# One stretch of hand order around the first expert, and later transposes for the next slot, in a fused attention and two-layer mixture kernel

## The chip, the cores and the metric

One Trainium2 chip, one of its cores. The metric is device time in microseconds (us) of one execution; lower is better.

## The reference, cut to what matters

```python
scores = cap * tanh(q @ k.T / sqrt(D) / cap)         # 4 batches, 12 heads, 448 tokens, D = 64
x = softmax(scores) @ v                              # 1792 tokens x 768
h = x @ w_in                                         # 768 -> 1024
x = layernorm(h * softmax(h)) * g_ln @ w_out         # 1024 -> 768
logits = x @ w_gate + modality_bias[modality_id]     # 8 experts
e_idx, gate = argmax(logits), its softmax weight
for e in range(8):                                   # only the chosen expert of each token
    out[e_idx == e] = gate * (relu(x @ w1[e]) @ w2[e])
```

## The kernel before, in words

Three parts follow one another on TensorE (PE): attention, the dense layer, and the routed experts. Products in full precision are made as three products of rounded halves (a high part `..h` and a low part `..l`), so each weight block needs two operations after its load: a cast on ScalarE (ACT) gives the high part, a subtraction on VectorE (DVE) the low part.

The experts run in slots. The first slot, **E**, takes 256 tokens of the expert that was most frequent in the early tokens, and it starts while the routing of the last tokens is being finished. Its first product is `e_h` (L1037): 6 blocks of the contraction times 8 column groups f times 3 matmuls, 144 in all. The sums lie in two tiles of PSUM, `e_ph0` (f 0 to 3) and `e_ph1` (f 4 to 7). In the last block, after each pair of column groups, ACT takes `e_hh = relu(e_ph)` (L1055) and DVE `e_hl` (L1056). Its second product is `e_o` (L1058): 8 steps f of 12 matmuls each, into the two tiles `e_po`. The weights of E come through `e_weights` (L1026): SyncE (SP) loads a block into `e_raw` (three buffers), ACT casts it (L1033), DVE subtracts (L1034). The second product has eight such blocks, k 0 to 7; block k 7 loads into the buffer that block k 4 leaves.

The next slot, **D**, takes 512 tokens of one expert. Four gathers on GpSimd (POOL) fetch its tokens (`ygD`, L1197). `s_tr` (L1203) transposes one of the four tiles with six PE transposes into two PSUM tiles `xtD` (L1219); ACT copies each to `xh_D` (L1220) and DVE makes `xl_D` (L1221). The pool `psT` for `xtD` has two buffers, so the next tile's transposes need the `xl_D` of the tile before. D's weight blocks are loaded by SP into `raw_D` (four buffers), and `c_split` (L1178) makes `wh_D` (ACT, L1188) and `wl_D` (DVE, L1189). A small slot **T** of 32 tokens runs inside D; its tokens are scaled on DVE (`t_sc`, L1338 to L1340) and then transposed on PE (`t_tr`, L1347).

All this is interleaved with `e_o` by `lead` (L1530): `e_o` calls `step(f)` ahead of the twelve matmuls of f. There `advance()` issues the next loads of D's weights and splits one block, and `tr(i)` makes the transposes of D's tile i (i = 4: `t_sc`, `t_tr` and one gather of T). `LTR` says at which f which `tr` is made.

The order of an engine's instructions comes from one of two sources. Inside `tc.manual_schedule(...)` the engines that are named (all, if none is named) keep the order in which the code is written. Outside, and on engines that are not named, a planner orders them by costs of its own. Each `manual_schedule` block is a stretch of its own, and the planner may interleave two neighbouring stretches. Before the change, the tail of the routing, all of `e_h` and E's weights form a stretch with hand order for PE and DVE alone, so ACT and SP are planned there. From `e_o` on, a second stretch has hand order on all engines:

```python
    with tc.manual_schedule(engines={ET.PE, ET.DVE}):
        ...
        for _ in eh:          # 102 matmuls of e_h that are left, with e_hh and e_hl
            pass
        for _ in ew:          # blocks k 4 to 7 of E's second product
            pass
    ...
    with tc.manual_schedule():
        next(slots)           # gathers and first loads of D, then lead
```

Of the kernel before, what the change touches and what calls it, by code (L numbers as in the profile page):

```python
# [25 lines left out]
ND = DM // P  # L26
# [12 lines left out]
COL0 = {"D": 0, "F": 16, "H": 32, "T": 40}  # L39
TT = 32  # L40
EARLY = 10
LTR = (2, 3, 4, 5, 7)
ENDS = (3, 4)
TAIL = (12, 12, 10)
NS = NK * len(KINDS)
# [41 lines left out]
def attn_moe_kernel(ctx, tc, qt, kt, vv, cap, w_in, w_out, g_ln, ids, w_gate, mbias, w1, w2, out):  # L87
# [949 lines left out]
    def e_h():  # L1037
        xh, xl = ee["xh"], ee["xl"]
        ph = []
        hh, hl = ([mp.tile([P, 4, SLOT], F32R, tag="m4", name=f"e_{x}{q}", bufs=4) for q in range(2)] for x in ("hh", "hl"))  # L1040
        ee["hh"], ee["hl"] = hh, hl
        for d in range(ND):
            for f in range(NF):
                if d == 0 and f % 4 == 0:
                    ph.append(atile(f"e_ph{f // 4}").rearrange("p a (b c) -> p (a b) c", c=SLOT))
                o = ph[f // 4][:, f % 4, :]
                c = slice(f * P, (f + 1) * P)
                pe.matmul(o, winh[d][:, c], xh[:, d, :], start=(d == 0 and f % 2 == 0), stop=False, skip_group_check=True)
                yield
                pe.matmul(o, winh[d][:, c], xl[:, d, :], start=False, stop=False, skip_group_check=True)  # L1050
                yield
                pe.matmul(o, winl[d][:, c], xh[:, d, :], start=False, stop=(d == ND - 1), skip_group_check=True)
                if d == ND - 1 and f % 2:
                    q, r = f // 4, slice(f % 4 - 1, f % 4 + 1)
                    act.activation(hh[q][:, r, :], ph[q][:, r, :], AF.Relu)  # L1055
                    dve.scalar_tensor_tensor(hl[q][:, r, :], ph[q][:, r, :], 0.0, hh[q][:, r, :], op0=ALU.max, op1=ALU.subtract)  # L1056
                yield
    def e_o(step):  # L1058
        po = [atile(f"e_po{i}") for i in range(2)]
        for f in range(NF):  # L1060
            step(f)
            for i in range(2):
                o = slice(i * P, (i + 1) * P)
                hh, hl = ee["hh"][f // 4][:, f % 4, o], ee["hl"][f // 4][:, f % 4, o]
                for hf in range(2):
                    c = slice(hf * HD, (hf + 1) * HD)
                    p = po[i][:, hf, :HD]
                    pe.matmul(p, hh, wouh[f][:, c], start=(f == 0), stop=False)
                    pe.matmul(p, hh, woul[f][:, c], start=False, stop=False)
                    pe.matmul(p, hl, wouh[f][:, c], start=False, stop=(f == NF - 1))  # L1070
        for i in range(2):
            ob = g2.tile([P, DM], F32, tag="tm", name=f"e_ob{i}", bufs=NTM)
            act.activation(ob[:, :HD], po[i][:, 0, :HD], AF.Copy, scale=ga0[:, i:i + 1])
            dve.tensor_scalar(ob[:, HD:], po[i][:, 1, :HD], ga0[:, i:i + 1], None, op0=ALU.mult)
            pool.indirect_dma_start(out=oview("E", i), out_offset=IndirectOffsetOnAxis(ap=sidx0[:, i:i + 1], axis=0),
                                    in_=ob, in_offset=None, bounds_check=NT, oob_is_err=False)
# [18 lines left out]
    def run(k):  # L1095
        for _ in range(k):
            msteps.pop(0)[1]()

    def run_h(k):
        for _ in range(k):  # L1100
            next(eh)

    def weights():
        yield from ee["w0"]
        yield from e_weights(1)

    with tc.manual_schedule(engines={ET.PE, ET.DVE}):
        run(4)
        ra, rb = (route_group(K, rt, psR, atile, *x) for x in groups)
        ew = weights()  # L1110
        next(ra)
        next(ew)
        run(5)
        next(ra)
        run(3)
        next(rb)
        next(ew)
        run(3)
        next(ra, None)
        run(3)  # L1120
        next(rb)
        next(rb)
        next(ew)
        run(4)
        eh = e_h()
        for steps, subs in EHS:
            run_h(steps)
            next(rb, None)
            for _ in range(subs):
                next(ew)  # L1130
        for _ in eh:
            pass
        for _ in ew:
            pass
    for pl_ in (rt, xp, wi, psR):
        pl_.release()

# [251 lines left out]
    def run_slots(seq, small, lead=None):  # L1389
# [63 lines left out]
        if lead:  # L1453
            lead(advance, first)
        else:
            s_tr(seq[0])
# [73 lines left out]
    def lead(advance, tr):  # L1530

        def step(f):
            if f < ND:
                advance()
            if f in LTR:
                tr(LTR.index(f))

        late["ps"] = psT
        e_o(step)
        for pl_ in (psT, psA, mp, wo):  # L1540
            pl_.release()
        late["g1"] = tc.alloc_tile_pool(name="g1", bufs=1, reuse_waits="tile")
        late["ps"] = tc.alloc_tile_pool(name="psC", bufs=8, space=PSUM, reuse_waits="tile")

    slots = run_slots(STATIC, SMALL, lead)
    with tc.manual_schedule():
        next(slots)
        more = nc.values_load(nsl[0:1, 4:5], min_val=0, max_val=4 * NK * len(KINDS))
        next(slots)
# [56 lines left out]
```

## Time and profile before

| | |
|---|---|
| median of 3 runs | 763.64 us |
| lowest run | 762.24 us |
| profiled execution | 764.74 us |
| span of the profile | 763.0 us |
| PE busy | 728.3 us (95% of the span) |
| DVE, ACT, POOL busy | 438.5, 387.2, 117.1 us |
| mean granted clock of PE | 0.982 |

The span goes from the first to the last instruction; the profiled execution's own time has 1.74 us around it. The granted clock is a share of 2.4 GHz: 1.00 is that level, 0.50 is 1.2 GHz. All times below count from the start of the span.

### The profile page before, as it was taken

How to read it: one execution, taken by the hardware profiler on the slowest of the kernel's cores; microseconds unless marked ns; L12 is line 12 of the kernel's file. 1: busy time of each engine (PE TensorE's matmuls, PEld its weight loads, DVE VectorE, ACT ScalarE, POOL GpSimd, SP SyncE). 2: the span in 40 equal slices, each digit the busy share in tenths (PEclk: the TensorE clock that was granted, in tenths of full speed). 3: DMA queues.
4: the chain of work that ended last, by engine and by line, in shares of the span. 5: the costliest groups of instructions: out<-in, count | busy, mean ns of one | idle time of the engine just before them, and what ended most of it. 6: DMA issues, size and time to landing. Idle time of an engine off the chain costs nothing. (4 is left out here: it accounts for less than half of the span.)

```text
span 763.0 us, 11321 instructions
## 1 busy us (share of the span) xinstructions
PE 728.3 (95%) x4302; PEld 560.6 (73%) x4302; DVE 438.5 (57%) x782; ACT 387.2 (51%) x535; POOL 117.1 (15%) x214
## 2 busy tenths in 40 slices
PE   6999999999999999999999999759999999999994
PEld 2434556666777777777698998759879998799983
DVE  7999556756655657554557458456147163563621
ACT  5899756775565555556522234234145162553530
POOL 4121101112021012111032111301200220002010
PEclk9999999999999999999999999978999999999998
DMA  9675211120121110100004022747927459584530
GB/s 303 233 248 184 61 57 47 56 80 36 37 82 37 58 57 28 44 34 13 22 21 146 22 77 70 234 160 252 383 85 247 154 158 395 221 259 163 204 107 22
DMA packets 33425, 97.13 MB, mean 127 GB/s; under 512 B 4903, under 2 KB 11057, under 8 KB 33362
## 3 DMA queue, kind: packets, MB, share of 16 engines
q1 hardware_dynamic: 26546, 66.88, 25.9%
q0 software_dynamic: 6528, 29.42, 10.9%
q8 instruction: 35, 0.57, 0.3%
q14 instruction: 28, 0.23, 0.1%
q10 hardware_dynamic: 288, 0.03, 0.0%
HBM read 85.24 MB, written 11.27 MB: 126 GB/s over the span
## 5 line engine op out<-in xcount | busy, mean ns | idle before, releaser
L735 ACT ACTIVATE e<-sc,sc 112x896 f32<-112x896 f32 x96 | 94.5, 1004 | 68.6 <-PE sc L728 68.6
L740 ACT ACTIVATE e<-e,cap_t 112x896 f32<-112x896 f32 x96 | 98.2, 1046 | 1.7
L770 PE MATMUL av<-e,v 112*64 112x448 f32 x384 | 83.3, 555 | 0.0
L650 PE MATMUL y<-wouh,lh 128*128 128x392 f32 (+1 forms) x224 | 77.9, 348 | 0.5 <-DVE lg L654 0.5
L652 PE MATMUL y<-wouh,ll 128*128 128x392 f32 (+1 forms) x224 | 75.8, 338 | 0.1
L651 PE MATMUL y<-woul,lh 128*128 128x392 f32 (+1 forms) x224 | 75.9, 339 | 0.0
L595 PE MATMUL h<-winh,xh 128*128 128x512 f32 x168 | 69.0, 410 | 0.0
L597 PE MATMUL h<-winh,xl 128*128 128x512 f32 x168 | 66.0, 393 | 1.1 <-DVE xl L583 1.1
L596 PE MATMUL h<-winl,xh 128*128 128x512 f32 x168 | 65.7, 391 | 0.0
L770 PEld LDWEIGHTS av<-e,v 112*64 112x64 f32 x384 | 23.3, 136 | 35.4 <-issue 33.1
L650 PEld LDWEIGHTS y<-wouh,lh 128*128 128x128 f32 x224 | 42.0, 188 | 9.1 <-issue 7.1
L1189 DVE TENSOR_TENSOR wl_H<-raw_H,wh_H 128x768 fp32r<-128x768 f32 (+1 forms) x28 | 29.2, 1069 | 32.9 <-ACT wh_H L1188 32.8
L595 PEld LDWEIGHTS h<-winh,xh 128*128 128x128 f32 x168 | 31.6, 188 | 16.5 <-issue 9.3
L1318 PE MATMUL poD<-wh_D,hhD 128*128 128x384 f32 x128 | 43.0, 336 | 0.0
L1319 PE MATMUL poD<-wl_D,hhD 128*128 128x384 f32 x128 | 42.8, 334 | 0.0
L1320 PE MATMUL poD<-wh_D,hlD 128*128 128x384 f32 x128 | 42.8, 334 | 0.0
L652 PEld LDWEIGHTS y<-wouh,ll 128*128 128x128 f32 x224 | 42.1, 188 | 0.8 <-DVE ll L640 0.8
L651 PEld LDWEIGHTS y<-woul,lh 128*128 128x128 f32 x224 | 42.1, 188 | 0.6
L1188 ACT CAST wh_H<-raw_H 128x768 fp32r<-128x768 f32 (+1 forms) x28 | 25.3, 943 | 33.1 <-PE phD L1246 15.2
L1189 DVE TENSOR_TENSOR wl_D<-raw_D,wh_D 128x768 fp32r<-128x768 f32 (+1 forms) x28 | 29.8, 1071 | 21.3 <-ACT wh_D L1188 21.1
L597 PEld LDWEIGHTS h<-winh,xl 128*128 128x128 f32 x168 | 31.5, 188 | 8.8 <-DVE xl L583 2.0
L1188 ACT CAST wh_D<-raw_D 128x768 fp32r<-128x768 f32 (+1 forms) x28 | 26.0, 931 | 23.6 <-DMA raw_D<-in_w_dram 23.4
(373 smaller groups left out, 1613.9 us busy)
## 6 DMA issues: line engine op xcount, KB each, us to landing
rawc<-in_w_out_dram POOLq DMA_DIRECT2D x16, 384.0 KB, 4.5
rawc<-in_w_in_dram POOLq DMA_DIRECT2D x12, 512.0 KB, 4.8
raw_D<-in_w_dram SPq DMA_DIRECT2D x12, 512.0 KB, 5.5
wr_T<-in_w_dram SPq DMA_DIRECT2D x16, 384.0 KB, 6.4
raw_D<-in_w_dram SPq DMA_DIRECT2D x16, 384.0 KB, 5.1
wr_T<-in_w_dram SPq DMA_DIRECT2D x12, 512.0 KB, 7.6
raw_H<-in_w_dram SPq DMA_DIRECT2D x12, 512.0 KB, 6.1
raw_H<-in_w_dram SPq DMA_DIRECT2D x16, 384.0 KB, 3.8
```

Source lines behind the costliest of these rows:

```text
L595: pe.matmul(o, s["xh"][d], winh[d][:, c], start=(d == 0), stop=False)
L596: pe.matmul(o, s["xh"][d], winl[d][:, c], start=False, stop=False)
L597: pe.matmul(o, s["xl"][d], winh[d][:, c], start=False, stop=(d == ND - 1))
L650: pe.matmul(o, s["lh"][f], wouh[f][:, c], start=(f == 0), stop=False)
L651: pe.matmul(o, s["lh"][f], woul[f][:, c], start=False, stop=False)
L652: pe.matmul(o, s["ll"][f], wouh[f][:, c], start=False, stop=(f == NF - 1))
L735: act.activation(e, t[:CK, :, :S], AF.Tanh, scale=sc8[:CK])
L740: act.activation(e, e, AF.Exp, scale=cap_t[:CK])
L770: pe.matmul(o[64 * j:64 * j + 64, :S], v[:, c, 64 * j:64 * j + 64], et[b, p, c][:, j, :], start=(c == 0), stop=(c == 3))
L1188: act.copy(h_, raw)
L1189: dve.tensor_sub(l_, raw, h_)
L1318: pe.matmul(p, hh[:, f, o], wh[:, c], start=(f == 0), stop=False)
```

## The change

The rest of `e_h` and of E's weights leaves the stretch with hand order on PE and DVE and opens the stretch with hand order on all engines, which then runs on without a break through `e_o` and the slots. In `lead`, D's four tiles are transposed at f = 3, 4, 5, 6 (before: 2, 3, 4, 5), T at 7 as before. `advance()` now stands behind `tr` and not ahead of it, and is called at f = 3 to 7 (five blocks) and not at f = 0 to 5 (six blocks).

```diff
-LTR = (2, 3, 4, 5, 7)
+LTR = (3, 4, 5, 6, 7)
...
-        for _ in eh:
-            pass
-        for _ in ew:
-            pass
+    hand = ExitStack()
+    hand.enter_context(tc.manual_schedule())
+    for _ in eh:
+        pass
+    for _ in ew:
+        pass
     for pl_ in (rt, xp, wi, psR):
         pl_.release()
...
         def step(f):
-            if f < ND:
-                advance()
             if f in LTR:
                 tr(LTR.index(f))
+            if f >= LTR[0]:
+                advance()
...
     slots = run_slots(STATIC, SMALL, lead)
-    with tc.manual_schedule():
+    with hand:
         next(slots)
```

## Rows read from the trace of the kernel before

**Rows 1.** Waits of PE, whole span: us in total, times, longest.

```profile
PE xtD L1219 <- DVE xl_D L1221: 8.5, 1, 8.5
...
PE e_po L1068 <- ACT e_hh L1055: 4.8, 1, 4.8
PE poH L1320 <- PEq L1558: 1.1, 1, 1.1
```

**Rows 2.** Timeline of PE, 490 to 496: start, us, operation, [idle before <-releaser].

```profile
490.53 0.28 PE L1050 MATMUL e_ph<-e_xl,winh 128*128 128x256 f32 x1
490.65 0.28 PE L1052 MATMUL e_ph<-e_xh,winl 128*128 128x256 f32 x1
495.74 0.69 PE L1068 MATMUL e_po<-wouh,e_hh 128*128 128x384 f32 x1 [4.82 <-ACT e_hh L1055]
```

**Rows 3.** Timeline of PE, 515 to 532.

```profile
515.52 1.54 PE L1219 MATMUL xtD<-ident,ygD 128*128 128x128 f32 x6 [8.45 <-DVE xl_D L1221]
...
520.64 0.82 PE L1219 MATMUL xtD<-ident,ygD 128*128 128x128 f32 x6
...
523.42 0.82 PE L1219 MATMUL xtD<-ident,ygD 128*128 128x128 f32 x6
...
530.71 0.34 PE L1069 MATMUL e_po<-woul,e_hh 128*128 128x384 f32 x1
...
531.06 0.39 PE L1245 MATMUL phD<-xh_D,wh_D 128*128 128x512 f32 x1
```

**Rows 4.** Timeline of PE's weight loads, around 496.

```profile
496.47 0.29 PEld L1048 LDWEIGHTS e_ph<-e_xh,winh 128*128 128x128 f32 x1 [0.23 <-DVE e_hl L1056]
```

**Rows 5.** Timeline of ACT, 494 to 522.

```profile
494.36 0.83 ACT L1033 CAST wouh<-e_raw 128x768 fp32r<-128x768 f32 x1 [1.68 <-DMA e_raw<-in_w_dram]
495.10 0.59 ACT L1055 ACTIVATE e_hh<-e_ph 128x512 fp32r<-128x512 f32 x1
...
507.43 0.83 ACT L1033 CAST wouh<-e_raw 128x768 fp32r<-128x768 f32 x1 [4.74 <-DMA e_raw<-in_w_dram]
508.78 1.05 ACT L1188 CAST wh_D<-raw_D 128x1024 fp32r<-128x1024 f32 x1 [0.52 <-DMA raw_D<-in_w_dram]
...
513.65 0.85 ACT L1220 CAST xh_D<-xtD 128x384 fp32r<-128x384 f32 x2
...
521.91 1.07 ACT L1188 CAST wh_D<-raw_D 128x1024 fp32r<-128x1024 f32 x1
```

**Rows 6.** Timeline of DVE, 495 to 527.

```profile
495.72 0.69 DVE L1056 SCALAR_TENSOR_TENSOR e_hl<-e_ph,e_hh 128x512 fp32r<-128x512 f32 x1 [10.10 <-ACT e_hh L1055]
...
503.33 2.68 DVE L1034 TENSOR_TENSOR woul<-e_raw,wouh 128x768 fp32r<-128x768 f32 x3
...
521.68 1.02 DVE L1221 TENSOR_TENSOR xl_D<-xtD,xh_D 128x384 fp32r<-128x384 f32 x2 [1.89 <-ACT xh_D L1220]
...
523.01 1.23 DVE L1189 TENSOR_TENSOR wl_D<-raw_D,wh_D 128x1024 fp32r<-128x1024 f32 x1 [0.25 <-ACT wh_D L1188]
...
525.67 0.11 DVE L1338 TENSOR_SCALAR gtT<-ygT 32x1 f32<-32x1 f32 x1
...
526.00 0.61 DVE L1340 TENSOR_SCALAR ygT<-ygT,gtT 32x768 f32<-32x768 f32 x1
```

**Rows 7.** Loads of E's weights: ns min/median/max, first and last issue.

```profile
L1031 SPq DMA_DIRECT2D e_raw<-in_w_dram x14: 332/333/374, 405.5 to 504.4; - x14
```

**Rows 8.** Loads of D's weights, all slots D: time to landing.

```profile
DMA to landing us min/median/max: 3.4/5.3/8.7
```

**Rows 9.** Windows: length, busy and count of PE, PEld, DVE, ACT, POOL; granted clock, DMA share, GB/s.

```profile
26.00:27.00 1.00, 1.00 (x8) 0.20 (x8) 1.00 (x4) 1.00 (x2) 0.38 (x1) 0.50 1.09 432
...
747.00:748.00 1.00, 0.48 (x3) 0.51 (x4) 0.00 (x0) 0.00 (x0) 0.00 (x0) 1.00 0.07 16
```

**Rows 10.** Windows of the D slot, columns as in rows 9.

```profile
552.00:554.00 2.00, 2.00 (x11) 1.65 (x10) 0.10 (x1) 1.05 (x1) 0.00 (x0) 1.00 1.02 412
...
558.00:560.00 2.00, 2.00 (x10) 1.65 (x10) 0.21 (x1) 0.76 (x2) 0.00 (x0) 1.00 0.01 4
```

## The prediction

> **What bounds the kernel now.** PE is busy for nearly the whole span, so only time that PE loses can be won. I read the list of PE's waits first: apart from the first load of the kernel, two entries matter, one of 8.5 us and one of 4.8 us, and both lie where the change works [rows 1]. Then the timeline of PE around them, for what stood in front and how fast PE ran behind, and last the timelines of the engines named as releasers.
>
> The first loss: after the 126th of `e_h`'s 144 matmuls (start 490.65) the next thing PE does is a matmul of `e_o` at 495.74, which waited 4.82 us for `e_hh` [rows 2]. `e_hh` could have run at 491, but on ACT it stands behind three casts of E's weights, the last of which itself waited for its load and started at 494.36; `e_hh` follows at 495.10 [rows 5]. The planner had put the casts first, since ACT is free of hand order there.
>
> The second: at f = 3 PE stands 8.45 us before D's second transposes, until `xl_D` of the first tile has freed the PSUM tiles; PE goes on at 515.52 [rows 3]. That `xl_D` waits for `xh_D` at 513.65, which on ACT is behind the casts of D's blocks 0 to 2 [rows 5], because `advance()` was called at f = 0, 1, 2 ahead of `tr(0)`. Those casts waited for loads: SP could issue them only behind E's last block (504.4) [rows 7], and that one only when DVE's subtraction of block k 4 (first of the three at 503.33 [rows 6]) had freed its buffer. So the late `e_hh` delays D's loads too.
>
> After either wait PE runs at the lower clock for a while: from 515.52 to 520.64 for six transposes and twelve matmuls that take 2.78 from 520.64 to 523.42 [rows 3], a loss of 2.34.
>
> **What can be won at most.** From 490.77 (where matmul 127 would have started: spacing 0.12, rows 2) to D's first product at 531.06 [rows 3] are 40.3 us. The work in it at full rate: 18 matmuls of `e_h` x 0.118 = 2.1; three steps f of `e_o` without transposes, 12 x 0.175 (two matmuls from 530.71 to 531.06, rows 3) = 2.1 each, 6.3; five steps with transposes, 2.78 each, 13.9. Sum 22.3, so 18.0 us are lost: 4.8 + 8.45 + 2.3 and, by difference, 2.4 behind the first wait.
>
> **What the change makes of it, part by part.**
>
> *One stretch on all engines.* ACT now takes the four `e_hh` ahead of the casts k 4 to 7. The 4.8 us go. But the planner could interleave two stretches, and within one it can't. Rows 4 show why it had moved two `e_o` matmuls into `e_h`: the next `e_h` matmul (f = 2, other bank of the same tile `e_ph0`) has a wait on `e_hl` of f = 0, 1; its weight load started 0.06 us after that `e_hl` ended (495.72 + 0.69 [rows 6]; 496.47 [rows 4]). In hand order nothing stands between. So PE stops at f = 2 of the last block and, in the other tile, at f = 6. Price of one: last matmul ends 490.93, `e_hh` 0.05 later, from its start to the weight load 1.37 (495.10 to 496.47), matmul 0.1 later, about 492.45 against 490.77: 1.65 us. Two: **3.3 us**. Bounds: 0, if the second is hidden by DVE and ACT order, to 3.6.
>
> Then `e_h` ends and `e_o` starts at 490.77 + 2.1 + 3.3, about 496.3. Its f = 0 needs the first `e_hh`, `e_hl`, long done. E's blocks: casts k 4 to 6 have their loads (the last cast began at 494.36 in the trace); they start behind the last `e_hh` at about 497.1. The subtraction of k 4 ends at 498.8 (2.68 for three, rows 6), SP issues k 7 at 498.9 and it lands 3.0 later (504.4 to 507.43, rows 5 and 7), at 501.9; its subtraction ends near 503.7, while `e_o` needs it at f = 7. No wait there, with some ten us of cover.
>
> *D's loads and transposes.* SP's first loads of D follow k 7; the first landed 4.4 after k 7's issue (508.78 [rows 5]), so now at 503.3 instead of 508.8. `tr(0)` comes at f = 3: 496.3 + 6.3 = 502.5. Per step f I take offsets from T, the start of its transposes (520.64 in the trace): `xl_D` at 1.04 to 2.06, cast of D's block from 1.27, subtraction 2.37 to 3.60 [rows 5, 6]. `xl_D` of tile 0 waits for k 7's subtraction and ends near 504.7; `tr(1)` is due at 505.3. Later steps come every 2.78 and each `xl_D` is done by T + 2.06: no PE wait as long as the subtraction (T + 3.60) leaves DVE before the next `xl_D` is due (T + 3.82). It does, by 0.2 us.
>
> *The move of `advance()` behind `tr`.* This has a price at f = 7, where `tr(4)` scales T's tokens on DVE before PE can transpose them. In the trace DVE was free for that at 525.67, long before. Now the subtraction of D's block 3, issued at f = 6, stands ahead: it ends at T6 + 3.60, the three T operations take 0.94 (525.67 to 526.61, rows 6), so T's transposes can start at T6 + 4.55 against T7 = T6 + 2.78: **1.8 us**, with the rest of `e_o` queued behind. Bounds 0 and 3 (a late block 3). The sixth block moves into D's first product, where it is needed five blocks later; nothing waits.
>
> *Behind `e_o`.* D starts at 496.3 + 6.3 + 13.9 + 1.8 = 518.3. T's blocks (SP) are released by `e_o`'s steps and so come earlier with them; D's blocks 4 and 5 fall 1 to 3 us later against `e_o`'s end. DMA is full there (share 1.02 at 552) but idle again at 558 [rows 10], and PE waited for no load in that slot [rows 1]. The two blocks are 1 MB, 2.5 us at the 412 GB/s of rows 10; I take 0, and 2.5 as the bound if the cover were gone.
>
> **Sum.** 18.0 - 3.3 - 1.8 = 12.9, rounded by the walk to 531.06 - 518.3 = 12.8. Profiled execution 764.74 - 12.8 = 751.9; it lay 1.1 above the median of 763.64, so on that scale **750.8 us**, 1.7% less. About 2% (15.3 us) is what a measurement of this kernel can tell from no change; the forecast is within it.
>
> **Rivals.** *The short stops cost the clock.* After the long waits PE came back at half rate and lost 2.3 to 2.4 each time. Against: a stop of 1.1 us near the end [rows 1] left the clock at 1.00 [rows 9]. For: at 26 the clock stood at 0.50 though PE shows no long gap [rows 9], and here two stops of 1.65 lie 1.4 us apart. One fall gives 753.1, a second, at f = 7, 755.5.
> The Trainium skill (TensorE: Matmul & The Clock Gate, "A second HAM failure mode: psum-queue depth-cycling") says that short idles of PE between groups of matmuls, from waiting for PSUM, can keep the clock going up and down; by that rule this rival is the likely one, and the trace has no such pair of stops to test it.
>
> *The stops are smaller.* If the waits at `e_ph` are not there, 747.5; if only T's is not, 749.0; neither, 745.7. For: the wait at f = 6 was already over when PE came to it in the trace. Against: rows 4.
>
> *D's loads come late and hold the transposes (the other side).* Place: ACT's cast of D's block 0 ahead of `xh_D` of tile 1. It must land by 504.7, 1.4 after my estimate; from there each us is a us of PE at `tr(2)`. With the longest landing of the trace, 8.7 [rows 8], it lands near 508.1: 754.2. Slower than before it gets from 12.8 us late on, at 517.5, twice the longest landing: possible only if the order on SP is otherwise than I read.
>
> *Nothing moves.* The planner keeps the casts ahead of `e_hh`, and the wait stays: 763.6.
>
> **How the numbers follow.** Forecast (749.5 to 752.5) 0.52; smaller stops 0.18; clock 0.18; late loads 0.08, of it 0.02 above 763.6; nothing moves 0.04. The range 747.5 to 755.5 takes in both stops' bounds and two falls of the clock. Faster by over 2% means below 748.4: most of the smaller stops, 0.15. Slower by over 2%: 0.02. Within: 0.83.
>
> **What would show it.** `e_hh` on ACT at 491, ahead of the three casts; two PE waits of about 1.5 for `e_hl`; D's loads from 499; no PE wait for `xl_D`; one of 1.8 at T's transposes; granted clock 1.00 through; D's product at 518. I am wrong if the `e_ph` waits are missing, if the clock falls, or if `xl_D` appears in the waits again.

## The result and the profile after

The changed kernel takes 752.36 us (median of 4 runs, 751.36 to 753.62) against 763.64 for the kernel before (median of 3 runs, 762.24 to 763.99), 11.3 less: ratio 0.9858, 95% interval 0.9834 to 0.9882. That is a gain of 1.2 to 1.7%, less than 2%. The forecast was 750.8, in a range of 747.5 to 755.5. The profiled execution took 751.36, its span 749.6 (before: 763.0). A fourth run of the kernel before, at 1039 us, is far off the others and is in no comparison.

The list of PE's waits in the changed kernel behind the kernel's first load, as in [rows 1] (us in total, times, longest):

```profile
PE e_ph L1048 <- DVE e_hl L1056: 2.8, 2, 1.4
PE tpT L1349 <- issue: 1.6, 1, 1.6
```

The two large waits of [rows 1] are gone, for `e_hh` (4.8) and for `xl_D` (8.5). In their place stand two stops for `e_hl` and one at T's transposes. PE's timeline, which answers to [rows 2 and 3]:

```profile
472.44 0.29 PE L1048 MATMUL e_ph<-e_xh,winh 128*128 128x256 f32 x1
...
488.84 0.28 PE L1052 MATMUL e_ph<-e_xh,winl 128*128 128x256 f32 x1
490.53 0.39 PE L1048 MATMUL e_ph<-e_xh,winh 128*128 128x256 f32 x1 [1.41 <-DVE e_hl L1056]
...
493.63 0.39 PE L1048 MATMUL e_ph<-e_xh,winh 128*128 128x256 f32 x1 [1.41 <-DVE e_hl L1056]
...
503.45 0.82 PE L1221 MATMUL xtD<-ident,ygD 128*128 128x128 f32 x6
504.03 0.42 PE L1068 MATMUL e_po<-wouh,e_hh 128*128 128x384 f32 x1
...
506.22 0.90 PE L1221 MATMUL xtD<-ident,ygD 128*128 128x128 f32 x6
...
511.64 0.34 PE L1070 MATMUL e_po<-wouh,e_hl 128*128 128x384 f32 x1
513.62 0.53 PE L1349 MATMUL tpT<-ident,ygT 32*128 32x32 f32 x6 [1.65 <-issue]
514.08 0.44 PE L1068 MATMUL e_po<-wouh,e_hh 128*128 128x384 f32 x1
...
517.63 0.60 PE L1247 MATMUL phD<-xh_D,wh_D 128*128 128x512 f32 x1
```

The steps with D's transposes follow one another without a stop (503.45, 506.22: 2.77). T's transposes stop PE, and the last twelve matmuls behind them are slow: 514.08 to 517.63 is 3.55, against 2.2 for the twelve from 504.03 to 506.22. The granted clock in windows shows why (columns as in [rows 9]):

```profile
26.00:27.00 1.00, 1.00 (x10) 0.16 (x8) 1.00 (x4) 1.00 (x2) 0.45 (x1) 1.00 1.05 414
512.00:514.00 2.00, 0.38 (x6) 0.41 (x6) 1.45 (x4) 0.00 (x0) 0.00 (x0) 1.00 0.87 238
514.00:516.00 2.00, 2.00 (x10) 1.96 (x9) 0.52 (x1) 1.31 (x3) 0.92 (x1) 0.66 0.97 389
516.00:518.00 2.00, 2.00 (x7) 1.96 (x7) 1.24 (x2) 0.66 (x2) 0.48 (x1) 0.50 1.03 413
546.00:548.00 2.00, 2.00 (x11) 1.65 (x10) 1.44 (x3) 1.75 (x4) 0.00 (x0) 1.00 0.01 2
```

The first row answers to the 0.50 at 26 in [rows 9]: here the clock stood at 1.00, and `e_h` begins 1.8 us earlier. Most of that is there long before the code that was changed: the dense layer's first matmul starts at 96.9, before at 98.6. It is why these two spans differ by 13.4 and the medians only by 11.3. The first matmul of `e_h` in the kernel before:

```profile
474.22 0.28 PE L1048 MATMUL e_ph<-e_xh,winh 128*128 128x256 f32 x1
```

For comparisons between profiles I therefore use the length from the first matmul of `e_h` to D's first product, called the **E-to-D length** below: before 474.22 to 531.06, 56.8; after 472.44 to 517.63, 45.2; **11.65 less**, close to the 11.3 of the medians. Each such length is from one profiled execution.

ACT, as in [rows 5]:

```profile
489.15 0.60 ACT L1055 ACTIVATE e_hh<-e_ph 128x512 fp32r<-128x512 f32 x1 [6.05 <-PE e_ph L1052]
...
495.14 2.29 ACT L1033 CAST wouh<-e_raw 128x768 fp32r<-128x768 f32 x3
...
503.28 1.05 ACT L1190 CAST wh_D<-raw_D 128x1024 fp32r<-128x1024 f32 x1 [0.61 <-DMA raw_D<-in_w_dram]
```

`e_hh` now waits for PE alone, and the three casts run in one piece behind the last `e_hh`. DVE and SP, as in [rows 6 and 7]:

```profile
489.79 0.69 DVE L1056 SCALAR_TENSOR_TENSOR e_hl<-e_ph,e_hh 128x512 fp32r<-128x512 f32 x1 [5.69 <-ACT e_hh L1055]
...
500.76 0.96 DVE L1034 TENSOR_TENSOR woul<-e_raw,wouh 128x768 fp32r<-128x768 f32 x1 [2.06 <-ACT wouh L1033]
...
505.50 1.02 DVE L1223 TENSOR_TENSOR xl_D<-xtD,xh_D 128x384 fp32r<-128x384 f32 x2
...
511.42 1.23 DVE L1191 TENSOR_TENSOR wl_D<-raw_D,wh_D 128x1024 fp32r<-128x1024 f32 x1
512.56 0.14 DVE L1340 TENSOR_SCALAR gtT<-ygT 32x1 f32<-32x1 f32 x1
...
512.91 0.61 DVE L1342 TENSOR_SCALAR ygT<-ygT,gtT 32x768 f32<-32x768 f32 x1
```

```profile
498.13 9.94 SPq L1177 DMA_DIRECT2D raw_D<-in_w_dram  x6
```

T's scaling ends at 513.52 and PE starts at 513.62; it begins only when the subtraction of D's block 3 is through. D's loads start at 498.13, before at 504.94.

### The profile page after: what moved, and what is told of

Same layout as the page of the kernel before. It is cut to its first block, busy times and chain, and to the rows that moved or that the text cites. A ratio compares the mean times of both kernels' runs of the same rounds, so it can differ in the third digit from the quotient of the medians.

```text
span 749.6 us, 11324 instructions
## 1 busy us (share of the span) xinstructions
PE 724.3 (97%) x4302; PEld 557.8 (74%) x4302; DVE 438.6 (59%) x782; ACT 387.1 (52%) x535; POOL 116.7 (16%) x214
```

## The experiments

Each ratio is to runs of the kernel before from the same series; their median was 763.58 in the first four experiments and 764.57 in the last four. So times of different series are compared by their ratios and not by their medians. "E to D" is the length defined above.

| | median, us | ratio to before, 95% interval | E to D, us |
|---|---|---|---|
| before | 763.64 | 1 | 56.8 |
| changed kernel | 752.36 | 0.9858 [0.9834, 0.9882] | 45.2 |
| merged stretch alone | 758.85 | 0.9931 [0.9907, 0.9955] | 52.0 |
| new lead alone | 756.29 | 0.9897 [0.9864, 0.9930] | 49.1 |
| T scaled early | 749.0 | 0.9807 [0.9773, 0.9841] | 42.6 |
| column order | 749.28 | 0.9817 [0.9775, 0.9858] | 41.4 |
| both | 747.72 | 0.9783 [0.9757, 0.9809] | 40.1 |
| split ahead of tr | 754.04 | 0.9869 [0.9833, 0.9904] | 47.6 |
| casts first | 758.16 | 0.9911 [0.9877, 0.9946] | 51.7 |
| no stop in `e_h` | 748.39 | 0.9787 [0.9762, 0.9813] | 39.4 |

**Merged stretch alone.** The changed kernel with the lead of before.

```diff
-LTR = (3, 4, 5, 6, 7)
+LTR = (2, 3, 4, 5, 7)
...
+            if f < ND:
+                advance()
             if f in LTR:
                 tr(LTR.index(f))
-            if f >= LTR[0]:
-                advance()
```

> The merged stretch alone, with the old lead (advance at f = 0 to 5 ahead of tr, tr at f = 2 to 5 and 7). My theory: e_hh runs ahead of the casts, so the first wait (4.8 us and its clock loss of 2.4) becomes two stops at e_ph of 1.65; but the copies of D's first tile again stand behind the casts of D's blocks 0 to 2, which now land 5.5 us earlier: PE waits about 6.8 us at f = 3 and loses 2.3 to the clock; no stop at T's transposes. About 758, half of the gain. Rival (the whole gain is in the later transposes): 763 to 764. Rival (the whole gain is in the merged stretch): 752.

Measured 758.85. PE's waits:

```profile
PE xtD L1221 <- DVE xl_D L1223: 6.9, 1, 6.9
...
PE e_ph L1048 <- DVE e_hl L1056: 2.8, 2, 1.4
```

The wait for `e_hh` is gone. The wait for `xl_D` stays, 1.6 shorter: counted from the first matmul of `e_h`, `xl_D` of D's first tile is done 5.3 us earlier than before, but PE comes to its wait 3.7 us earlier too. So neither part is the whole gain.

**New lead alone.** The kernel before with the new `LTR` and the new order in `step`.

```diff
-LTR = (2, 3, 4, 5, 7)
+LTR = (3, 4, 5, 6, 7)
...
-            if f < ND:
-                advance()
             if f in LTR:
                 tr(LTR.index(f))
+            if f >= LTR[0]:
+                advance()
```

> The new lead alone (tr at f = 3 to 7, advance behind it), with the two stretches as before. My theory: the 4.8 us wait for e_hh and its clock loss stay, no stops of 1.65 at e_ph; the wait of 8.45 at f = 3 falls to about 1, with no clock loss behind it; T's transposes are stopped for 1.8 and may cost the clock 1.5. About 756 to 757.5. Rival (transposes late only help with loads that come early): the wait for xl_D stays at 3 us or more, 759 or above. Rival (whole gain in the lead): 752.

Measured 756.29.

```profile
PE e_po L1068 <- ACT e_hh L1055: 5.3, 1, 5.3
PE tpT L1347 <- issue: 1.6, 1, 1.6
...
PE xtD L1219 <- DVE xl_D L1221: 1.2, 1, 1.2
```

The wait for `e_hh` stays, no stop for `e_hl` appears, and the wait of 8.45 shrinks to 1.2. In the E-to-D length the two parts give 4.8 and 7.8, 12.6 together, and 11.65 when both are made: nearly additive. With both there is one fall of the clock that neither profile of a part has at T's stop.

**T scaled early.** In the changed kernel `t_sc` moves from `tr(4)` to the end of `tr(3)`, ahead of the split at f = 6.

```diff
             if i < len(cols(seq[0])):
                 s_tr(seq[0], (i,))
+                if smalls and i == len(cols(seq[0])) - 1:
+                    t_sc(smalls[0])
             elif smalls:
-                t_sc(smalls[0])
                 t_tr(smalls[0])
```

> The changed kernel, with the scaling of T's tokens on DVE ahead of the last split and not behind it. My theory: the stop of 1.8 us at T's transposes is DVE's queue and goes, and with it the fall of the clock behind it (1.4 to 1.7): 749.0, 3.4 less than the changed kernel. Rival (the stop is something else, T's gather or the PSUM tile): no change, 752.4. Rival (the fall of the clock comes from the two stops at e_ph and not from this one): 750.6, with a fall still in the trace between 490 and 520.

Measured 749.0.

```profile
PE e_ph L1048 <- DVE e_hl L1056: 2.8, 2, 1.4
...
PE tpT L1349 <- issue: 0.4, 1, 0.4
```

The profile names no releaser for T's stop ("issue"); this experiment shows that 1.3 of its 1.65 us were DVE's queue. The E-to-D length is 2.6 shorter: 1.3 of the stop, and 1.35 of a clock that does not fall in this profile (1.00 from 480 to 520).

**Column order.** In the changed kernel the last block of `e_h` takes its column groups in another order.

```diff
-            for f in range(NF):
+            for f in range(NF) if d < ND - 1 else (0, 1, 4, 5, 2, 3, 6, 7):
```

> The changed kernel, with the column groups of e_h's last block in the order 0, 1, 4, 5, 2, 3, 6, 7, so that the other PSUM tile is worked on while ACT and DVE read the first. My theory: the stop of 1.65 is the wait for e_hl of the same tile; the first shrinks to about 1.0, the second goes: 2.3 less, 750.1; T's stop stays at 1.8. Rival (the wait is on ACT and DVE in general, not on the tile): two stops as before, 752.4.

Measured 749.28.

```profile
PE tpT L1349 <- issue: 1.7, 1, 1.7
...
PE e_ph L1048 <- DVE e_hl L1056: 0.7, 1, 0.7
```

One of the two stops is gone and the other has halved, as a wait on the tile demands. The clock is the surprise: T's stop is as long as in the changed kernel, and in this profile the clock stays at 1.00 behind it. The four runs spread from 747.86 to 752.43 us, with mean clocks from 0.996 down to 0.989, so the clock differs between executions of this one kernel too.

```profile
512.00:514.00 2.00, 1.34 (x11) 1.33 (x12) 0.56 (x1) 0.77 (x2) 0.53 (x1) 1.00 0.94 330
514.00:516.00 2.00, 2.00 (x12) 1.91 (x11) 1.47 (x2) 1.52 (x3) 0.39 (x1) 1.00 1.02 386
```

**Both.** T scaled early and the column order, the two edits above together.

> The early scaling of T's tokens and the column order 0, 1, 4, 5, 2, 3, 6, 7 together, in the changed kernel. My theory: the stops are separate and add up: 3.4 and 2.3 to 3.1 off the changed kernel's 752.4, 746.7, ratio to the kernel before 0.978; no fall of the clock between 480 and 520. Rival (PE that comes sooner meets D's loads or the subtractions of DVE, a new wait for xl_D): 748 to 749.

Measured 747.72, a us above the 746.7 expected; the profiled execution took 745.97.

```profile
PE e_ph L1048 <- DVE e_hl L1056: 0.7, 1, 0.7
...
PE tpT L1349 <- issue: 0.4, 1, 0.4
```

No new wait for `xl_D`, no fall of the clock from 480 to 520. The E-to-D length is 5.1 below the changed kernel's; single edits gave 2.6 and 3.8, and each of those counts the one fall of the clock, so they overlap by it (1.35).

**Split ahead of tr.** The changed kernel with the two calls in `step` exchanged.

```diff
+            if f >= LTR[0]:
+                advance()
             if f in LTR:
                 tr(LTR.index(f))
-            if f >= LTR[0]:
-                advance()
```

> The changed kernel, with advance ahead of tr again (still from f = 3 on, five blocks). My theory: each tile's copies now stand behind a cast and a subtraction on ACT and DVE: PE waits about 1 us at f = 4 for xl_D of the first tile, and T's scaling stands behind one more subtraction, so its stop is 3 us or more with a clock loss of 1.5 to 2.3: 754.5 to 756.5. Rival (only the later f matters, and not the order of the two calls): 752.4.

Measured 754.04, a little under the 754.5 to 756.5 expected.

```profile
503.69 1.04 ACT L1190 CAST wh_D<-raw_D 128x1024 fp32r<-128x1024 f32 x1 [2.42 <-DMA raw_D<-in_w_dram]
504.64 0.85 ACT L1222 CAST xh_D<-xtD 128x384 fp32r<-128x384 f32 x2
```

```profile
PE xtD L1221 <- DVE xl_D L1223: 2.6, 1, 2.6
PE tpT L1349 <- issue: 1.6, 1, 1.6
```

The wait for `xl_D` comes back, 2.6 and not about 1: on ACT the first tile's `xh_D` stands behind the cast of D's first block, and that cast waits for its load. T's stop stays at 1.6, where I expected 3: that part of the expectation was wrong. The order of the two calls is worth 2.4 us in the E-to-D length; the ratios, 0.9869 and 0.9858, do not tell the two kernels apart. The rest of the new lead's gain comes from the later start of `tr` and of `advance` together, which no run takes apart.

**Casts first.** The changed kernel with blocks k 4 to 6 of E's weights written ahead of the rest of `e_h`.

```diff
+    for _ in range(3):
+        next(ew)
     for _ in eh:
         pass
     for _ in ew:
         pass
```

> The changed kernel, with blocks k 4 to 6 of E's weights written ahead of the rest of e_h, so that their casts stand ahead of e_hh on ACT and their subtractions ahead of e_hl on DVE in hand order. My theory: this is the order that cost the kernel before its first wait: e_hh again waits for the load of k 6, PE stands about 4.5 us longer at f = 2 and loses 2.3 to the clock: 758 to 760, though D's loads come earlier. Rival (the first wait came from the planner's interleaving of e_o into e_h, not from the casts): 752 to 753.

Measured 758.16.

```profile
492.74 0.83 ACT L1033 CAST wouh<-e_raw 128x768 fp32r<-128x768 f32 x1 [1.87 <-DMA e_raw<-in_w_dram]
493.47 0.59 ACT L1055 ACTIVATE e_hh<-e_ph 128x512 fp32r<-128x512 f32 x1
```

```profile
PE e_ph L1048 <- DVE e_hl L1056: 7.3, 2, 5.9
```

`e_hh` again follows the third cast, which again waits for its load, and one stop grows from 1.4 to 5.9. In one stretch of hand order, with no `e_o` matmul between those of `e_h`, the wait of before is back: the order of casts and `e_hh` on ACT made it. This edit changes DVE's order as well; there the subtraction of k 6 (493.60 to 494.56) holds `e_hl` for some 0.4 us of the 5.9.

**No stop in `e_h`.** T scaled early, and the last two blocks of `e_h` interleaved, so that at least 12 matmuls lie between the reading of a tile and its next writing.

```diff
-        for d in range(ND):
-            for f in range(NF):
+        order = [(d, f) for d in range(ND - 2) for f in range(NF)]
+        order += [(d, f) for d, fs in ((4, (0, 1)), (5, (0, 1)), (4, (4, 5, 6, 7)), (5, (4, 5)), (4, (2, 3)), (5, (2, 3, 6, 7))) for f in fs]
+        for d, f in order:
```

> The early scaling of T's tokens, and e_h's last two blocks interleaved by column group (block 4 of 0, 1; block 5 of 0, 1; block 4 of 4 to 7; block 5 of 4, 5; block 4 of 2, 3; block 5 of 2, 3, 6, 7), so that 12 matmuls lie between a tile's reading and its next writing. My theory: no stop at e_ph is left: 1.0 below the version with both edits, 745.7. Rival (the 1.4 us of 12 matmuls are too short, or the weights of the last block too late): 746.7 or above.

Measured 748.39, above the version with both edits; by the expectation's number that is the rival's. But what the rival said does not stand in the trace. A view of the weight loads of PE from 470 to 530:

```profile
PEld e_ph L1049 <- DVE e_hl L1057: 0.2, 1, 0.2
```

The stop in `e_h` is gone but for 0.2, and the E-to-D length is the shortest of all, 39.4, 0.7 below the version with both edits. The profile lost its time in the attention part, which these edits do not touch: `e_h` began at 475.8 and not at 472.4, and the clock was lower there (in the version with both edits it was 1.00 in both of these windows).

```profile
25.00:30.00 5.00, 5.00 (x25) 1.50 (x24) 4.61 (x16) 3.16 (x6) 0.53 (x1) 0.75 0.71 256
35.00:100.00 65.00, 64.59 (x396) 28.72 (x394) 52.18 (x104) 55.57 (x80) 10.48 (x17) 0.97 0.50 157
```

All six of its runs have a mean clock of 0.991 to 0.993 (0.994 to 0.997 for the version with both edits). Only one of the six was profiled: whether the others lost it in attention too is not shown, and why was not tried. The version with both edits has the lowest ratio to the kernel before, 0.9783 [0.9757, 0.9809], and this one, at 0.9787, is not to be told apart from it by the total.

## Why the prediction was right

*The 18 us at stake.* From the 127th matmul to D's first product there were 40.3 us before. After: `e_hh` starts at 489.15, some 0.03 behind the end of the 126th matmul, and the 127th was due at 488.96 (488.84 + 0.12); to 517.63 that is 28.7. The sum of work was 22.3, so 6.4 are still lost: 3.1 at the two stops (1.57 each), 1.8 at T's, 1.35 to the clock, and 0.1 that I can't place.

*`e_hh` ahead of the casts.* Right. Merging alone removes the wait, writing the casts first brings it back.

*Two stops at `e_ph`, 3.3.* Right in place, cause and size: the 127th matmul was due at 488.96 and started at 490.53, 1.6 late, and the second stop is as long (3.1 in all); another column order leaves 0.7 of the two waits of 1.4.

*E's block k 7 and D's loads.* The subtraction of k 7 was forecast to end at 503.7, in this profile's time 501.9; it ended at 500.76 + 0.96 (DVE), 501.7. D's first block came later than thought: it was due at 503.3, here 501.5, and ACT took it at 503.28. The margin of 1.4 us that I gave it was used up, and PE still did not wait. The rule for `tr(2)` was too strict: PE began those transposes at 506.22, while the pair of `xl_D` that frees the two PSUM tiles ran from 505.50 to 506.52. That fits if the first three transposes need only the first of the two tiles. The rival of late loads did not come, but it was nearer than its 0.08 says; when `advance` stands ahead of `tr` it costs 2.6.

*T's stop, 1.8.* Right: due at 511.64 + 0.18, started at 513.62, 1.8. Moving three DVE operations takes 1.3 of it away.

*The cover behind `e_o`.* Right: PE waits for no load in slot D, and DMA is idle again at 546 to 548.

*The size that was off.* The sum gave the clock nothing for the short stops, "granted clock 1.00 through" was a sign to be seen, and a fall was one of my signs of being wrong; it came. In the changed kernel's profile the clock fell behind T's stop: 1.35 us on the last twelve matmuls and some 0.2 on D's first. 12.8 less 1.6 is 11.2; the medians say 11.3. I had this as a rival with 0.18, at 2.3 for one fall; it is what happened in this profile, with 1.6.

The reason that I gave for it, two stops in a row, is not what the profile shows: the clock was at 1.00 through both stops at `e_ph` and fell after the single one at T. The fall near 26 that I named for it had a short stop too, of 0.34 us at 24 (last section), which I had not seen. And it isn't T's stop alone: the profiles of the new lead alone, the column order and the casts first have the same stop of 1.6 to 1.7 with no fall behind it. Of five profiles with T's stop two show a fall, the changed kernel and the one with the split ahead, which has a stop of 2.6 for `xl_D` as well. The four runs of the changed kernel have mean clocks of 0.994, 0.991, 0.994 and 0.991, the lower two at 753.62 and 752.59 us, the others at 751.36 and 752.13; only the first, at 751.36, was profiled, and a mean does not say where a clock fell. That the other three runs miss the forecast by this same fall is not shown, and since executions also differ by some us in attention (below), it is partly luck that the median lies so close to the sum. What decides whether the clock falls stays open.

The Trainium skill (TensorE: Matmul & The Clock Gate, "A second HAM failure mode: psum-queue depth-cycling"), whose rule I set against the change, speaks of many short idles of PE between groups of matmuls, where PE cycles through the banks of PSUM, and of a clock that goes up and down by them. No run here shows it: the two stops at `e_ph` are the nearest thing to it, and behind them the clock stayed at 1.00 in all four profiles that have both at 1.4 us, while the stop at T is a wait for DVE's scaling.

## What to carry to other kernels

When a planner orders one engine and the code another, look for the small operation on the way of PE that the planner put behind work that waits for loads; here its price was the whole wait for the load, 4.8 us, and the clock behind it. Here a PSUM tile that is read in parts and written in parts made PE stop for the reading, 1.6 us at each of two places, and working on the other tile in between took one line. When a call that feeds three queues is moved, walk each queue past the next thing that PE needs: here the gain of 8.5 us left a stop of 1.8 behind, three DVE operations too late.

## What the runs showed of the hardware that was not expected

The granted clock of PE differs between executions in a part that no edit touches. Near 26 us it stood at 0.50 in the kernel before and at 1.00 in the changed one. PE was busy in that window in both, but not two us ahead of it. The transposes of attention at 24, first in the kernel before, then in the changed one:

```profile
24.08 0.55 PE L543 MATMUL pt<-ident,to 128*128 128x128 f32 x3 [0.34 <-ACT e L735]
```

```profile
24.01 0.53 PE L543 MATMUL pt<-ident,to 128*128 128x128 f32 x3
```

Of the ten profiles, four have this stop, of 0.34 to 0.74 us: the kernel before, the merged stretch alone, the column order and no stop in `e_h`. The same four have a low clock behind it, 0.56 to 0.60 on average from 25 to 28. The other six have no stop there, and 1.00. So in this stage a stop of 0.34 us came ahead of a fall, while the two stops of 1.4 us in `e_h` had none behind them. This is what ten profiles have in common and not an experiment; why ACT was late in those four is not shown.

`e_h` began between 472.4 and 475.8 in the ten profiles. That is 0.4% of the time, as much as some of the edits here, and a difference of spans between two profiles takes it in.
